# First guess of 1/Q in a PSUM bank: MoE1's reciprocal without VectorE operations on two SBUF operands

## The chip, the cores and the metric

The kernel runs on one core of a Trainium2 chip. The metric is the device time of one launch in microseconds. The engines are TensorE (PE, with its weight loads listed as PEld), VectorE (DVE), ScalarE (ACT), GpSimd (POOL) and SyncE (SP, which only issues DMAs here). Each engine runs its own instructions in the order in which the program wrote them, and waits on semaphores for the others. SBUF is the large on-chip memory, PSUM the small one into which TensorE writes its products.

## The reference

Three layers follow each other on 2304 tokens of width 512:

```
x = attention(q, k, v)                      # 4 batches, 8 heads, local and strided masks
h = x @ w_in                                # MoE1: 512 -> 2048
P = a0 + a1 h + a2 h^2 + a3 h^3
Q = 1 + |b0| |h| + |b1| h^2
x = (P / (Q + 1e-6)) @ w_out                # 2048 -> 512
out = gate * (relu(x @ w1[e]) @ w2[e])      # MoE2: e = the token's best expert of 8
```

All is float32. The products of MoE1 and MoE2 are made of three products each, with every operand split into a high part, which TensorE takes at full speed, and a low part, the rest.

## The kernel before

MoE1 is a pipeline over 96 steps. Step s is one block of 384 tokens (s // 16, six blocks) and one chunk of 128 hidden units (s % 16). One step is:

- **m1** (line 499): 12 matmuls of 384 columns into one of the two PSUM banks of tag "h".
- **fA** (446, 447), ScalarE: A = |h|, and G = a line in h, both to SBUF.
- **fP** (451, 452), GpSimd: Q = (b1 A + b0) A.
- **fD**, **fE** (457, 462), VectorE: G = G h and G = (G + a1) h. The h here is read from PSUM, and after fE its bank is free.
- **rA** (466, 467), ScalarE: A = Ln(Q + c), then A = Exp(-A): the first guess of 1/Q. The constant c is 1 + 1e-6.
- **rD**, **rN**, **rG** (471, 475, 479), VectorE: Q = (Q + c) A, Q = (Q - 2) A (one Newton step), G = (G + a0) Q.
- **sA** (383), ScalarE: gh, the high part of G. **sP** (489), GpSimd or VectorE: gl = G - gh.
- **m2** (510): 9 matmuls of 512 columns into three PSUM banks of tag "o".

The tiles A, Q, G, gh and gl have two buffers each. The order in which the program writes its operations is an order written by hand: `PLAN` has one line of operation names for each phase, and a window takes it through two steps. An entry such as `rA@-1` in window w means "go on with rA to step 2w - 1", and it is passed over where `ready` says that what it needs has not been written yet; a later entry of the same name then catches up. The phases are "first" (windows 0 to 7), "plain" (8 to 14), "attention" (15 to 31) and "last" (from 32). Attention of the first batch runs ahead of step 0, that of the second within steps 0 to 15, and that of the last two within steps 30 to 63. So steps 16 to 29 and 64 to 95 have no attention beside them. What they have is the router of MoE2 (rT, rE, rL, rP, rQ, rB: TensorE transposes and small products, with evacuations by ScalarE and VectorE), in the last phase also the sorting of tokens by expert (`rank`, `star_keys`, `star_slots`) and the splitting of MoE2's first weights (`w_unit`, lines 1097 and 1098).

In the phase "plain" one window is written as

```
m2@-3 rA@-1 m1@0 fA@0 xA.A@-2 sc@0 rD@-1 rN@-1 rG@-1 fP.G@0 ae.A@-1 lq@0 sA.A@-1 m1@1 mid@0 fD@0
fE@0 mx@0 rL@1 rP.A@1 rE.D@1 sP.D@-1 qk.A@1 rA@0 rT@0 m2@-2 rB@0 rD@0 rN@0 rG@0 mid@1 tail@1 aT@0
fA@1 fD@1 fE@1 sA.A@0 tail@0 rc@0 fP.G@1 end@1 xD@-1 nm.G@0 pv@0 sP.G@0 ex.A@0 end@0 rQ@1
```

All other PSUM work after the start-up (transposes, scores, router) takes its bank from `misc`, which goes round three banks of tag "m". A bank taken with a name is held until `release` of that name; `can_alloc(k)` says whether the next k banks in the round have been released, and `ready` asks it for the operations that need one.

Of the kernel before, what the change touches and what calls it, by code (L numbers as in the profile page):

```python
# [19 lines left out]
def tile_attention_moe_moe2(  # L20
# [86 lines left out]

# [1 line left out]
    pairs = [(b, hp) for b in range(B) for hp in (0, 2, 1, 3)]  # L109
# [51 lines left out]

# [1 line left out]
    ident = const.tile([128, 128], F32, name="ident")  # L163
# [19 lines left out]

    # coefficients: columns 0-3 = -a, 4-5 = |b|, 6 = 1 + 1e-6
    coef = const.tile([128, 8], F32, name="coef")
# [5 lines left out]

# [1 line left out]
    wi = w_in.bitcast(U32).rearrange("(k p) w -> p k w", p=128)  # L193
# [72 lines left out]

# [1 line left out]
    qkT = {}  # L268
# [30 lines left out]
    def emit_scores(U):  # L299
        n, hf = UN[U]  # L300
        hp = pairs[n][1]
        nq, nk, cnt = shape_of(U)
        qT, kT = qkT[n, "q"], qkT[n, "k"]
        banks = [misc('sc'), misc('sc')]
        where = {}
        for c in range(cnt):
            for j in range(2):
                if hp < 2:
                    # rows: head j's d; columns: position
                    r, o = j, c * nk  # L310
                    q0 = 96 * (hf * cnt + c)
                    k0 = max(q0 - 32, 0)
                else:
                    # rows: d for even or odd residues; columns: head, residue pair, position
                    r, o = c % 2, (2 * j + c // 2) * nk
                    q0 = k0 = 288 * hf + o
                PE.matmul(
                    banks[r][0:nq, o : o + nk],
                    lhsT=qT[64 * r : 64 * r + 64, q0 : q0 + nq],
                    rhs=kT[64 * r : 64 * r + 64, k0 : k0 + nk],  # L320
                    start=True, stop=True,
                )
                where[c, j] = banks[r][0:nq, o : o + nk]
        sc_t[U] = where
# [108 lines left out]

# [1 line left out]
    xs = dram.tile([NT, XW], F32, name="xs")  # L435
    hid = {}
    st = {}
# [21 lines left out]
    def ew_p2(s):  # L459
        A, Q, G = st[s]  # L460
        h = hid.pop(s)
        DVE.scalar_tensor_tensor(out=G, in0=G, scalar=coef[:, 1:2], in1=h, op0=ALU.add, op1=ALU.mult)  # L462

    def ew_recip(s):
        A, Q, G = st[s]
        ACT.activation(out=A, in_=Q, func=ACTF.Ln, bias=coef[:, 6:7])  # L466
        ACT.activation(out=A, in_=A, func=ACTF.Exp, scale=-1.0)  # L467

    def ew_newton(s):
        A, Q, G = st[s]  # L470
        DVE.scalar_tensor_tensor(out=Q, in0=Q, scalar=coef[:, 6:7], in1=A, op0=ALU.add, op1=ALU.mult)  # L471

    def ew_newton2(s):
        A, Q, G = st[s]
        DVE.scalar_tensor_tensor(out=Q, in0=Q, scalar=2.0, in1=A, op0=ALU.subtract, op1=ALU.mult)  # L475

    def ew_ratio(s):
        A, Q, G = st[s]
        DVE.scalar_tensor_tensor(out=G, in0=G, scalar=coef[:, 0:1], in1=Q, op0=ALU.add, op1=ALU.mult)  # L479

# [31 lines left out]

# [1 line left out]
    wg = px.tile([128, KD * E + 32 - E], F32, name="wg")  # L514
# [34 lines left out]
    def route_mm(i, t):  # L549
        """Parts of the logits: rows 32 k to 32 k + 7 for the k-th 128 of the model dimension (other rows unused)."""  # L550
        xT = x2t[i, t, "s"]
        m = x2t[i, t, "P"] = misc("rL")
        for kk in range(KD):
            PE.matmul(m[32 * kk : 32 * kk + 32, 0:128], lhsT=wg[:, E * kk : E * kk + 32],
                      rhs=xT[:, 128 * kk : 128 * kk + 128], start=True, stop=True, tile_position=(0, 32 * kk))
# [18 lines left out]
    def first_max(dst, src, n):  # L574
        """dst <- one-hot of the first maximum along the last axis of src [128, n, E]; returns src - max."""
        mx = px.tile([128, n, 1], F32, tag="mx", name="mx", bufs=2)
# [31 lines left out]

# [1 line left out]
    NU = len(UN)  # L610
# [5 lines left out]

    # The order of the work: one line of operations for each phase, as name[.engine]@offset. In the start-up an
    # operation goes on to attention unit (or weight group) u + offset; later, a window is two steps of MoE1, and an
    # operation goes on to step 2 w + offset, or to the unit of window w + offset.
    # MoE1: m1 m2 products, fA fP fD fE polynomials, rA rD rN rG reciprocal and ratio, sA sP high and low part of the result.  # L620
    # Attention: qk q and k transposed, sc scores, mx maximum, ex exponential, rc nm division by the sum, aT ae transposed
    # weights, pv values, xA xD high and low part of the result. c0A c0P c1 c1b c2A c2P: conversion of weights; lw, lq, ln:
    # loads; rT rE rL rP rQ rB: router; x0 x1 y0 y1: start of MoE2's first tile; kw: idle products; mid, tail, end: work of MoE2's routing.
    PLAN = {
# [33 lines left out]
    PLAN = {name: list(parse(text)) for name, text in PLAN.items()}  # L658
    CV = (1, 0, 2, 1, 2, 1, 3, 1, 2, 4, 1)   # weight units whose conversion starts, by iteration of the start-up
    LD = (2, 6, 0, 0, 0, 6, 0, 2, 1, 0, 0)   # weight units whose load starts  # L660
    KW = ((13, 0, 0), (0, 2, 11), (0, 1, 5), (1, 2, 4), (2, 0, 3), (6, 0, 2), (0, 3, 9), (0, 9, 0), (5, 3, 7), (8, 7, 0), (0, 9, 4))
    B0 = 1

# [1 line left out]
    NS = NBLK * NF  # L665
# [26 lines left out]
    def ready(T, j):  # L692
# [21 lines left out]
        elif T == "aT":  # L714
            return can_alloc(2)
        elif T in ("pv", "rL", "rQ"):
            return can_alloc(1)
# [48 lines left out]
    def releasing(f, kind, n):  # L766
# [6 lines left out]
        "x0": lambda j: x_T(0), "x1": lambda j: x_evac(0), "y0": lambda j: up(0, 0), "y1": lambda j: up(0, 1),  # L773
        "m1": mm1, "fA": ew_abs, "fP": ew_q, "fD": ew_p, "fE": ew_p2, "rA": ew_recip, "rD": ew_newton, "rN": ew_newton2, "rG": ew_ratio, "sA": ew_high,
        "sP": lambda s, eng: ew_low(s, DVE if s == NS - 1 else eng), "m2": run_m2, "sc": emit_scores, "mx": releasing(emit_max, "sc", 2), "ex": emit_exp,
# [95 lines left out]

# [1 line left out]
    R = {}  # L873
# [36 lines left out]
    def cols(x, n, m):  # L910
        """x [128, n] seen as [128, n, m]."""
        return x.rearrange("p (n o) -> p n o", o=1).to_broadcast([128, n, m])

    def rows(x, n, m):
        """x [128, m] seen as [128, n, m]."""
        return x.rearrange("p (o m) -> p o m", o=1).to_broadcast([128, n, m])
# [12 lines left out]
    def rank(i, eng):  # L929
        """Rank of each token among its expert's tokens, as (row of 128, place in it)."""  # L930
        rank_mm(i)
# [21 lines left out]
    def choose():  # L953
        """The expert with the most tokens so far: its weights are loaded early."""
        s = small_t([128, 1, E], "star")
# [13 lines left out]
    def reserve():  # L969
        """Tile 0 takes the chosen expert's tokens up to here; later ones start at tile 1."""  # L970
        c = R["cum"][:, 15]
        DVE.scalar_tensor_tensor(out=c, in0=R["s"], scalar=float(TILE), in1=c, op0=ALU.mult, op1=ALU.max)

    def index_tiles(m, n, name):
        """m [128, 2n] in PSUM: place + 1, and token tile, of each slot (0: empty) -> gather and scatter rows."""
        vv, v, z = small_t([128, 2 * n], name + "vv"), small_t([128, n], name + "v"), small_t([128, n], name + "z")
# [8 lines left out]
    def star_keys(i0, i1):  # L985
        """Rows of 128 of the chosen expert's tokens, others negative, for blocks i0 to i1 - 1."""
        tt, n = slice(3 * i0, 3 * i1), 3 * (i1 - i0)
# [10 lines left out]
    def star_slots(a, i0, i1):  # L998
        """Columns of tile a (0 or 1): place + 1, and token tile, of blocks i0 to i1 - 1."""
        tt = slice(3 * i0, 3 * i1)  # L1000
# [51 lines left out]
    def experts():  # L1052
        """Expert of each tile, and the number of tiles."""
        m, b = R["tiles"]
# [21 lines left out]
    def load_e(t, k):  # L1076
        """Expert weights of tile t, matrix k (1 or 2), as four slots."""
        e = R["e", t]
# [55 lines left out]
    def hidden(t, f):  # L1134
        """High and low part of a chunk of the hidden units; the first of tile 0 lie where MoE1's last block was."""
        if t == 0 and f < KD:
# [54 lines left out]

    # the router's later half inside MoE1
    last = NBLK - 1
    at_step(end, 63, route_setup)
    def spread(s0, g, every=1):
        """One part of g per step, from step s0 on."""
        def part():
# [158 lines left out]
```

## Time and profile before

| what | value |
|---|---|
| median of 3 runs | 891.7 us (891.23 to 892.05) |
| span of the profiled execution, from its first to its last instruction | 887.6 us |
| median of the runs less that span | 4.1 us |
| busy share of the span: PE, DVE, ACT, POOL | 91%, 82%, 60%, 54% |
| mean granted TensorE clock | 0.964 of full |

The profile is that of one execution. Its span leaves out what lies ahead of the first and behind the last instruction, so it stands below the runs' times. Matmuls are pipelined: each is listed with some 340 to 400 ns, but the next one starts before it ends, so that the distance from start to start, not the listed duration, is what a matmul costs.

### The profile page before, as it was taken

What the parts mean: (1) busy time and instruction counts of PE and PEld (TensorE: products, weight loads), DVE (VectorE), ACT (ScalarE), POOL (GpSimd) and SP (SyncE); (2) the same over time, 40 slices, a digit from 0 to 9 for tenths busy, and PEclk for the clock granted to TensorE, in tenths of its full rate; (3) what the DMA queues carried; (4) which work ended last, traced back from release to release, by engine and by line L of the source; (5) the groups of instructions that cost most, each with busy time, mean ns of one, the idle gap of its engine ahead of it and who ended that gap; (6) DMA issues with size and microseconds to landing.
All of it is one profiled execution on the core that took longest, in us unless ns stands there. A gap on an engine that the chain in (4) does not pass through costs nothing.

```text
span 887.6 us, 15602 instructions
## 1 busy us (share of the span) xinstructions
PE 804.6 (91%) x5294; PEld 677.4 (76%) x5301; DVE 730.9 (82%) x1656; ACT 534.4 (60%) x1397; POOL 476.8 (54%) x463
## 2 busy tenths in 40 slices
PE   6787787889999999999999988997899999999995
PEld 3555676767878788888788867886679999999994
DVE  5899999889897988788988999889966677777772
ACT  4776676565556887888776545555542555555552
POOL 3786878785554444443446667666613444444431
PEclk9888898899999999999999999999999999999998
DMA  8991241102000211131000000302014877776730
GB/s 197 304 271 47 75 126 45 31 8 64 8 1 28 80 44 35 27 105 35 20 15 25 12 1 1 131 1 97 24 38 114 340 238 232 226 232 223 231 120 5
DMA packets 71609, 85.59 MB, mean 96 GB/s; under 512 B 38111, under 2 KB 48607, under 8 KB 71520
## 3 DMA queue, kind: packets, MB, share of 16 engines
q1 hardware_dynamic: 68112, 74.36, 27.6%
q0 software_dynamic: 3120, 10.13, 3.4%
q8 instruction: 44, 0.72, 0.3%
q14 instruction: 45, 0.37, 0.1%
q10 hardware_dynamic: 288, 0.00, 0.0%
HBM read 74.89 MB, written 9.85 MB: 95 GB/s over the span
## 4 chain that ended last, share of the span: by engine, by line
PE 38%; DVE 29%; ACT 12%; POOL 8%; issue 6%; DMA 3%; SPq 2%; another core or an unknown queue 0%; DVEq 0%; POOLq 0%; ACTq 0%
PE h L1147 12%; PE o L1161 11%; DVE G L479 7%; DVE Q L475 6%; PE h L499 5%; PE o L510 5%; DVE Q L471 5%; ACT S L353 3%; ACT A L466 3%; ACT A L467 3%; POOL Q L452 3%; POOL Q L451 2%; DVE G L457 1%; POOL S L370 1%; DVE G L462 1%
## 5 line engine op out<-in xcount | busy, mean ns | idle before, releaser
L499 PE MATMUL h<-xh,wi 128*128 128x384 f32 x768 | 221.5, 351 | 7.5 <-DVE G L462 7.0
L510 PE MATMUL o<-wo,gh 128*128 128x512 f32 x576 | 190.9, 413 | 4.3 <-ACT gh L383 2.4
L451 POOL TENSOR_SCALAR Q<-A,coef 128x384 f32<-128x384 f32 x96 | 86.0, 896 | 163.5 <-ACT A L446 163.2
L499 PEld LDWEIGHTS h<-xh,wi 128*128 128x128 f32 x768 | 145.1, 194 | 13.8 <-DVE G L462 11.0
L499 PE MATMUL h<-xl,wi 128*128 128x384 f32 x384 | 132.1, 344 | 4.7 <-DVE xl L432 4.7
L510 PEld LDWEIGHTS o<-wo,gh 128*128 128x128 f32 x576 | 106.1, 192 | 30.7 <-ACT gh L383 6.3
L510 PE MATMUL o<-wo,gl 128*128 128x512 f32 x288 | 118.4, 411 | 5.5 <-POOL gl L489 3.2
L452 POOL TENSOR_TENSOR Q<-Q,A 128x384 f32<-128x384 f32 x96 | 111.8, 1164 | 8.0
L383 ACT CAST gh<-G 128x384 fp32r<-128x384 f32 x96 | 49.2, 512 | 103.9 <-DVE G L479 103.7
L489 POOL TENSOR_TENSOR gl<-G,gh 128x384 fp32r<-128x384 f32 x71 | 74.7, 1052 | 46.6 <-ACT gh L383 43.3
L471 DVE SCALAR_TENSOR_TENSOR Q<-Q,coef,A 128x384 f32<-128x384 f32 x96 | 66.0, 688 | 33.7 <-ACT A L467 23.1
L479 DVE SCALAR_TENSOR_TENSOR G<-G,coef,Q 128x384 f32<-128x384 f32 x96 | 90.7, 945 | 3.4
L1147 PE MATMUL h<-xh,w1h 128*128 128x256 f32 x320 | 89.7, 280 | 1.6 <-DVE G L462 1.6
L1147 PE MATMUL h<-xh,w1l 128*128 128x256 f32 x320 | 89.1, 278 | 0.0
L1147 PE MATMUL h<-xl,w1h 128*128 128x256 f32 x320 | 88.9, 278 | 0.0
L1151 ACT ACTIVATE hh<-h 128x256 fp32r<-128x256 f32 x76 | 29.2, 384 | 98.9 <-PE h L1147 98.9
L353 ACT ACTIVATE S<-S,nb 72x72 f32<-72x72 f32 (+1 forms) x224 | 80.6, 363 | 6.8 <-DVE nb L340 6.8
L466 ACT ACTIVATE A<-Q,coef 128x384 f32<-128x384 f32 x96 | 59.0, 615 | 36.6 <-POOL Q L452 36.5
L499 PEld LDWEIGHTS h<-xl,wi 128*128 128x128 f32 x384 | 74.8, 195 | 6.6 <-DVE xl L432 5.0
L475 DVE SCALAR_TENSOR_TENSOR Q<-Q,A 128x384 f32<-128x384 f32 x96 | 76.9, 801 | 3.3
L510 PEld LDWEIGHTS o<-wo,gl 128*128 128x128 f32 x288 | 55.5, 193 | 26.7 <-POOL gl L489 9.7
L1152 DVE SCALAR_TENSOR_TENSOR hl<-h,hh 128x256 fp32r<-128x256 f32 x76 | 32.2, 424 | 39.7 <-ACT hh L1151 39.7
(208 smaller groups left out, 1879.0 us busy)
## 6 DMA issues: line engine op xcount, KB each, us to landing
w1r<-in_moe_w_dram SPq DMA_DIRECT2D x36, 512.0 KB
w2r<-in_moe_w_dram SPq DMA_DIRECT2D x36, 512.0 KB
rawi<-in_moe_w_in_dram SPq DMA_DIRECT2D x16, 512.0 KB
rawo<-in_moe_w_out_dram SPq DMA_DIRECT2D x16, 512.0 KB
xs<-x SPq DMA_DIRECT2D x18, 256.0 KB
vt<-in_v_dram SPq DMA_DIRECT2D x48, 64.0 KB
rawq<-in_q_dram SPq DMA_DIRECT2D x16, 144.0 KB
rawk<-in_k_dram SPq DMA_DIRECT2D x16, 144.0 KB
```

The costliest lines, as they stand in the source:

```text
L353: ACT.activation(out=Sv[:, j, c], in_=Sv[:, j, c], func=ACTF.Exp, scale=-1.0, bias=nb[0:nq, u : u + 1], **({"accum_out": rb[0:nq, u : u + ...
L451: eng.tensor_scalar(out=Q, in0=A, scalar1=coef[:, 5:6], scalar2=coef[:, 4:5], op0=ALU.mult, op1=ALU.add)
L452: eng.tensor_tensor(out=Q, in0=Q, in1=A, op=ALU.mult)
L466: ACT.activation(out=A, in_=Q, func=ACTF.Ln, bias=coef[:, 6:7])
L471: DVE.scalar_tensor_tensor(out=Q, in0=Q, scalar=coef[:, 6:7], in1=A, op0=ALU.add, op1=ALU.mult)
L475: DVE.scalar_tensor_tensor(out=Q, in0=Q, scalar=2.0, in1=A, op0=ALU.subtract, op1=ALU.mult)
L479: DVE.scalar_tensor_tensor(out=G, in0=G, scalar=coef[:, 0:1], in1=Q, op0=ALU.add, op1=ALU.mult)
L489: eng.tensor_tensor(out=gl, in0=G, in1=gh.bitcast(F32), op=ALU.subtract)
L499: PE.matmul(h[:, 0:BLK], lhsT=w[:, o + 128 * kk : o + 128 * kk + 128], rhs=x[:, kk, c0 : c0 + BLK], start=n == 0, stop=n == 11)
L510: PE.matmul(acc[t], lhsT=a[:, ts], rhs=w[:, o : o + 512], start=f == 0 and n == 0, stop=f == NF - 1 and n == 2)
L1147: PE.matmul(h, lhsT=w[kk][:, 128 * f : 128 * f + 128], rhs=x[:, kk, c0 : c0 + TILE], start=n == 0, stop=n == 11)
L1161: PE.matmul(acc, lhsT=a[:, hs], rhs=w[f // 2][:, ws], start=f == 0 and n == 0, stop=f == NH - 1 and n == 2)
```

## The change

In steps 16 to 29 and 64 to 95 (46 of 96) `ew_recip` takes a bank of tag "m" under the name "y", and the Exp writes the first guess y there instead of into A. The three VectorE operations are written in another order of factors: G = (G + a0) y, then y = (Q + c) y within the bank, then G = (y - 2) G, after which the bank is released. The number of operations, their kinds, their sizes and their engines stay as they were. Each of the three now has one tensor operand in PSUM and one in SBUF, and the second one also writes to PSUM. In `ready`, rA of such a step asks for a free bank, and rD, which now needs G, for fE of its step. The other 50 steps keep the old form, and `PLAN` is not touched. The rest of the diff takes out comments.

```
+    def y_in_psum(s):
+        return 16 <= s < 30 or s >= 64
+
     def ew_recip(s):
         A, Q, G = st[s]
         ACT.activation(out=A, in_=Q, func=ACTF.Ln, bias=coef[:, 6:7])
-        ACT.activation(out=A, in_=A, func=ACTF.Exp, scale=-1.0)
...
+        y = misc("y")[:, 0:BLK] if y_in_psum(s) else A
+        ACT.activation(out=y, in_=A, func=ACTF.Exp, scale=-1.0)
+        st[s] = y, Q, G
+
+    def ew_1(s):
+        y, Q, G = st[s]
+        if y_in_psum(s):
+            DVE.scalar_tensor_tensor(out=G, in0=G, scalar=coef[:, 0:1], in1=y, op0=ALU.add, op1=ALU.mult)
+        else:
+            DVE.scalar_tensor_tensor(out=Q, in0=Q, scalar=coef[:, 6:7], in1=y, op0=ALU.add, op1=ALU.mult)
+
+    def ew_2(s):
+        y, Q, G = st[s]
+        if y_in_psum(s):
+            DVE.scalar_tensor_tensor(out=y, in0=Q, scalar=coef[:, 6:7], in1=y, op0=ALU.add, op1=ALU.mult)
+        else:
+            DVE.scalar_tensor_tensor(out=Q, in0=Q, scalar=2.0, in1=y, op0=ALU.subtract, op1=ALU.mult)
+
+    def ew_3(s):
+        y, Q, G = st[s]
+        if y_in_psum(s):
+            DVE.scalar_tensor_tensor(out=G, in0=y, scalar=2.0, in1=G, op0=ALU.subtract, op1=ALU.mult)
+            release("y")
+        else:
+            DVE.scalar_tensor_tensor(out=G, in0=G, scalar=coef[:, 0:1], in1=Q, op0=ALU.add, op1=ALU.mult)
...
-        elif T in ("pv", "rL", "rQ"):
+        elif T == "rD":
+            return not y_in_psum(j) or done["fE"] > j
+        elif T in ("pv", "rL", "rQ") or (T == "rA" and y_in_psum(j)):
             return can_alloc(1)
...
-        "m1": mm1, "fA": ew_abs, "fP": ew_q, "fD": ew_p, "fE": ew_p2, "rA": ew_recip, "rD": ew_newton, "rN": ew_newton2, "rG": ew_ratio, "sA": ew_high,
+        "m1": mm1, "fA": ew_abs, "fP": ew_q, "fD": ew_p, "fE": ew_p2, "rA": ew_recip, "rD": ew_1, "rN": ew_2, "rG": ew_3, "sA": ew_high,
```

## Rows read from the trace of the kernel before

**Rows 1.** Windows: stretch, length; busy us (count) of PE, PEld, DVE, ACT, POOL; clock, DMA.

```profile
210.00:280.00 70.00, 66.50 (x347) 55.39 (x346) 60.78 (x98) 39.74 (x84) 36.16 (x36) 0.98 0.11 32
478.00:600.00 122.00, 115.62 (x607) 95.37 (x605) 110.51 (x199) 66.50 (x139) 81.20 (x86) 1.00 0.09 31
600.00:645.00 45.00, 36.80 (x195) 29.75 (x195) 42.80 (x88) 25.79 (x53) 28.85 (x27) 1.00 0.19 60
```

**Rows 2.** Chain that ended last, one step of block 1: start, us, what.

```profile
247.07 0.40 issue
247.47 0.62 ACT A L466
...
248.11 0.54 ACT A L467
...
248.74 0.63 DVE Q L471
...
249.39 0.92 DVE Q L475
...
250.34 1.25 DVE G L479
```

**Rows 3.** Timeline of DVE and POOL: start, us, engine, line, operation.

```profile
249.98 1.20 POOL L452 TENSOR_TENSOR Q<-Q,A 128x384 f32<-128x384 f32 x1
...
275.53 0.62 DVE L479 SCALAR_TENSOR_TENSOR G<-G,coef,Q 128x384 f32<-128x384 f32 x1
...
276.12 0.66 POOL L451 TENSOR_SCALAR Q<-A,coef 128x384 f32<-128x384 f32 x1 [1.91 <-ACT A L446]
```

**Rows 4.** One line's instructions: shortest, median and longest in ns, first and last start.

```profile
L462 DVE SCALAR_TENSOR_TENSOR G<-G,coef,h x96: 601/614/617, 86.2 to 640.1; 128x384 f32<-128x384 f32 x96
...
L1152 DVE SCALAR_TENSOR_TENSOR hl<-h,hh x76: 410/425/426, 655.3 to 871.7; 128x256 fp32r<-128x256 f32 x76
```

**Rows 5.** Timeline of PE around 590 us: start, us, engine, line, operation, count.

```profile
586.14 0.60 PE L539 MATMUL m<-ident,x 128*128 128x128 f32 x4
...
586.76 0.34 PE L499 MATMUL h<-xl,wi 128*128 128x384 f32 x1
...
588.49 0.34 PE L499 MATMUL h<-xh,wi 128*128 128x384 f32 x1
...
589.69 0.40 PE L510 MATMUL o<-wo,gl 128*128 128x512 f32 x1
...
593.19 0.40 PE L510 MATMUL o<-wo,gl 128*128 128x512 f32 x1
```

**Rows 6.** PE busy time (count) in the stretches of rows 1: line 499, then line 510.

```profile
210.00:280.00 70.00, 30.63 (x163) 0.98 0.11 32
478.00:600.00 122.00, 56.40 (x296) 1.00 0.09 31
600.00:645.00 45.00, 13.86 (x72) 1.00 0.19 60
...
210.00:280.00 70.00, 33.94 (x126) 0.98 0.11 32
478.00:600.00 122.00, 58.97 (x225) 1.00 0.09 31
600.00:645.00 45.00, 19.47 (x74) 1.00 0.19 60
```

**Rows 7.** A PE wait at 266 us (timeline), and PE and its clock just after (windows).

```profile
266.46 1.06 PE L290 MATMUL m<-ident,rawk 72*128 72x72 f32 x8 [0.85 <-ACT x2T L383]
...
268.00:269.00 1.00, 1.00 (x4) 0.50 0.54 70
```

**Rows 8.** DVE busy time (count) from 600 to 645 us: lines 471, 475, 479.

```profile
600.00:645.00 45.00, 5.77 (x8) 1.00 0.19 60
...
600.00:645.00 45.00, 5.55 (x8) 1.00 0.19 60
...
600.00:645.00 45.00, 7.84 (x8) 1.00 0.19 60
```

More of the change, by code (lines that the diff above doesn't have):

```diff
@@ L466, in ew_recip @@
         ACT.activation(out=A, in_=Q, func=ACTF.Ln, bias=coef[:, 6:7])
-        ACT.activation(out=A, in_=A, func=ACTF.Exp, scale=-1.0)
[L469 to L479, printed above, removed]
+        y = misc("y")[:, 0:BLK] if y_in_psum(s) else A
[20 more added lines that the diff above has]
+            DVE.scalar_tensor_tensor(out=G, in0=G, scalar=coef[:, 0:1], in1=Q, op0=ALU.add, op1=ALU.mult)
     def ew_high(s, eng=ACT):
```

## The prediction

> **What bounds the kernel now.** I read the table of stretches first, then the chain of waits inside one stretch, then the timeline of two engines, and last the counts of matmuls.
>
> The 46 changed steps lie in two places: steps 16 to 29 between 210 and 280 us, and steps 64 to 95 between 478 and 645 us. There VectorE is busy 60.8 of 70, 110.5 of 122 and 42.8 of 45 us [rows 1]. TensorE looks full in the same rows (66.5 of 70), but a listed matmul overlaps the next, so its busy time hides short waits. From start to start it costs less: between 586.76 and 588.49 us lie ten starts of 384 columns, 0.173 us each; between 589.69 and 593.19 fifteen of 512 columns, 0.233 us each [rows 5]. A step of MoE1 (12 and 9 of them) is thus 12 x 0.173 + 9 x 0.233 = 4.18 us of TensorE at best.
>
> The chain of waits shows why a step takes longer than that. Near 247 us it never touches TensorE: ScalarE casts G of one step (sA), then takes the Ln and Exp of the next (rA), VectorE does rD, rN and rG, and the cast of that step waits for rG. ScalarE's order is sA(s), rA(s+1), fA(s+2), sA(s+1), so this is a closed loop. From the cast's wait at 247.07 to rD at 248.74 pass 1.67 us; the three VectorE operations last until 250.34 + 1.25 = 251.59, 2.85 us; 0.05 us pass to the next cast: 4.57 us a step [rows 2], against 4.18 of TensorE.
>
> In that loop rN takes 0.92 and rG 1.25 us [rows 2]. The same rG at 275.53 us, where POOL idles (its next operation starts at 276.12 after 1.91 us of idleness), takes 0.62; the slow rG runs beside POOL's multiplication of 249.98, 1.20 us long [rows 3]. So VectorE and GpSimd hold each other up where both read from SBUF. VectorE's operations with one operand in PSUM don't suffer: fE (line 462), of the same kind and size, stays within 601 to 617 ns in all 96 cases, and line 1152, whose first operand is in PSUM and whose second is in SBUF, within 410 to 426 in 76 [rows 4], although POOL is busy for over half of the span.
>
> **The change part by part.** *The three VectorE operations.* The new rD is fE's form to the letter (SBUF tensor, coefficient, PSUM tensor): 0.61 us. The new rG is line 1152's form with 384 columns instead of 256. I price each of the three at 0.62, the free rG [rows 3], and 0.65 with the gap behind it: 1.95 us for 2.85. The loop becomes 1.67 + 1.95 + 0.05 = 3.67 us, under TensorE's 4.18, so in a step without other work TensorE is next to bind.
>
> *Writing to PSUM.* The Exp and the middle operation write to PSUM, which no ScalarE or VectorE row here does. From below: the fastest similar operation is line 1152's 0.43 us, which would change little, since TensorE binds already. From above I take the contended rG, 1.25 us [rows 2]: the loop is then 3.67 + 0.63 = 4.30. I take 0.62, because reading PSUM costs nothing extra (0.61 in fE against 0.62 from SBUF [rows 3, 4]); both ends stay in the range. The Exp by itself has over half a microsecond of room (4.18 - 3.67).
>
> [...]
>
> *The bank.* y holds one of three "m" banks from rA to rG. Of the entries between these two in the plan, none in "plain" or "last" takes more than one bank (rT, one `rank` product) before rG releases y, and in the phase "last" rE gives rT's bank back before the next rA; the two banks of x0 are asked for after one y, with the other two free. So I find no place where rA is put off. The real wait is that an Exp writes where three allocations earlier another user sat: mostly y of two or three steps before, whose rG is over long since. Behind a late Exp would queue fA and sA of ScalarE, and for these VectorE and POOL. In window 14 the second q transpose takes the bank of y(27), so TensorE now waits there for rG(27); but the evacuations of these transposes already stand behind sA(27), which needs the same rG, and that is why TensorE waits 0.85 us at 266 us [rows 7]. No wait is new in length.
>
> *rD after fE.* fE(s) is written ahead of rD(s) in every window of both phases, so the condition is always met. Costs nothing.
>
> *POOL.* Its operations lose the same collisions: 1.20 us for the Q product [rows 3]. It isn't in the loop: no gain counted. DMAs are not touched.
>
> *The sum*, by how much TensorE waits in each stretch. The floor is the counts of matmuls [rows 6] times 0.173 and 0.233; the other matmuls get 0.08 us each (four transposes and a product lie between 586.14 and 586.76, so 0.11 each; one product, eight small ones and two of 512 columns between 588.49 and 589.69, so 0.07 each [rows 5]).
> - 210 to 280: 163 x 0.173 + 126 x 0.233 + 58 x 0.08 = 62.2, so 7.8 us of waiting. After the wait at 266 us the granted clock is at its lower level, 0.50 or 1.2 GHz [rows 7], and eight matmuls take about twice as long: some 1.6 us, which I leave standing, with half of the wait ahead of it, 0.7. Gain 5.5.
> - 478 to 600: 296 x 0.173 + 225 x 0.233 + 86 x 0.08 = 110.5, so 11.5 us. VectorE sheds 25 x 0.9 = 22 us at most, far more than that. But routing work sits in the chains of VectorE and POOL here, and its waits don't go. I take 70%, my choice: 8.0.
> - 600 to 645: 72 x 0.173 + 74 x 0.233 + 49 x 0.08 = 33.6, so 11.4 us. Here VectorE is full (42.8 of 45 [rows 1]), with the splitting of weights on it. The three lines take 5.77 + 5.55 + 7.84 = 19.2 us [rows 8]; eight steps at 3 x 0.62 are 14.9. VectorE still binds, and the gain is what it sheds: 4.3.
>
> Together 17.8 us. Nothing later gives it back: attention and MoE2 keep their code and simply start earlier. Against the span of 887.6 that is 869.8; the runs stand 4.1 us above the span, so the median goes from 891.7 to about 874.0.
>
> **The rivals.**
> *The writes are dear* (rN near 1.25 us). The loop is 4.30 instead of 4.57: 14 x 0.27 = 3.8 us in the first stretch, 25 x 0.27 = 6.8 in the second, cut by the same 70% to 4.7, and 4.3 - 8 x 0.63 = -0.7 in the third: 7.8 us, 884. For it: no row of such a write. Against it: reading is free of any extra.
>
> *Slower: writes into PSUM that cost more than the collisions did.* Place: the Exp and rN, both in the loop. The point that decides is 2.85 - 1.95 = 0.90 us a step more than I priced; at 1.2 us more, 46 x 0.3 = 13.8 us are lost: 905.5. Against it: it would need a threefold price for an operation whose read side shows none.
>
> *No change: TensorE binds already.* For it: near 590 us, with router work between the products, its starts follow each other without a gap [rows 5]. If all steps were like that, faster VectorE would only wait longer, and the time would stay within 1.8 us of 891.7. Against it: 7.8 + 11.5 + 11.4 = 30.7 us in which TensorE waits.
>
> *All waiting goes*, the clock's dip and the routing's waits with it: at most 30.7, say 27 us: 864.7.
>
> **How the numbers follow.** The forecast, with a gain of 11 to 25 us (867 to 881), gets 0.70; dear writes 0.12; all waiting gone 0.06; no change 0.05; slower 0.07. The range 864 to 885 takes in the forecast, the dear writes at the upper bound and most of the largest gain; it leaves out some 0.15. A measurement here can tell about 0.2%, 1.8 us, from no change. Faster by more: 0.70 + 0.12 + 0.06 = 0.88; same 0.05; slower 0.07.
>
> **What the profile after would show.** Right: rG and rN of the changed steps at 0.56 to 0.65 us whether or not POOL works beside them; the chain between 210 and 265 us through TensorE instead of lines 471 to 479; VectorE's busy share there down from 87% to about 75%; TensorE's waits for fE and gl shorter; steps 30 to 63 as they were. Wrong: an Exp well over 0.54 us or a middle operation over 1 us; an Exp waiting for a bank; a new dip of the clock; or waits of the routing chain in 478 to 645 us as long as now, so that the second and third gains shrink.

## The result, and the profile after

The changed kernel takes 865.8 us (864.46 to 866.58), beside 891.47 for the kernel before in the same comparison: a ratio of 0.9711, with a 95% interval of 0.9698 to 0.9725, so 25.7 us less. The forecast was 874.0 us, 17.8 less. The direction and the mechanism held, and the time lies inside the stated range of 864 to 885. But it lies 1.2 us below the forecast's own range (867 to 881), and the case nearest to it is the one in which all waiting goes (864.7).

The page of the changed kernel: busy time of each engine, and the chain that ended last, by engine and by line.

```profile
PE 793.3 (92%) x5301; PEld 678.0 (79%) x5301; DVE 688.3 (80%) x1656; ACT 536.6 (62%) x1397; POOL 464.1 (54%) x463
...
PE 55%; DVE 19%; ACT 11%; POOL 7%; issue 4%; DMA 2%; SPq 0%; another core or an unknown queue 0%; POOLq 0%; DVEq 0%; ACTq 0%
PE h L516 13%; PE o L527 12%; PE h L1166 12%; PE o L1180 11%; ACT S L353 4%; DVE G L496 3%; DVE Q L488 2%; POOL Q L452 2%; DVE Q L481 2%; POOL Q L451 2%; ACT A L470 2%; POOL S L370 1%; ACT A L472 1%; PE m L379 1%; PE zb L632 1%
```

The same line of the chain on the page of the kernel before:

```profile
PE 38%; DVE 29%; ACT 12%; POOL 8%; issue 6%; DMA 3%; SPq 2%; another core or an unknown queue 0%; DVEq 0%; POOLq 0%; ACTq 0%
```

TensorE's part of the chain rose to 55%, from 38%, and VectorE's fell to 19%, from 29%.

The table of stretches, with the columns of [rows 1]. Each window now reaches from the start of one step's Ln to that of another (steps 16 to 30, 64 to 88, 88 to 95), so that both kernels are compared over the same steps. The kernel before:

```profile
209.50:277.91 68.41, 64.91 (x336) 53.78 (x335) 59.47 (x96) 38.18 (x78) 35.21 (x36) 0.98 0.12 32
480.68:600.72 120.04, 113.31 (x596) 93.26 (x594) 108.55 (x199) 66.49 (x139) 79.82 (x85) 1.00 0.09 32
600.72:640.43 39.71, 32.25 (x172) 26.12 (x170) 37.89 (x78) 22.57 (x47) 27.61 (x27) 1.00 0.21 68
```

The changed kernel:

```profile
210.21:271.63 61.42, 60.86 (x336) 53.20 (x335) 46.32 (x96) 38.83 (x78) 30.81 (x36) 1.00 0.13 36
474.75:581.56 106.81, 106.72 (x587) 93.10 (x587) 86.76 (x199) 67.87 (x139) 72.79 (x85) 1.00 0.10 36
581.56:616.40 34.84, 32.98 (x185) 28.44 (x184) 33.46 (x78) 22.64 (x45) 25.93 (x27) 1.00 0.23 77
```

In the first two VectorE is now busy for 75% and 81% of the time (87% and 90% before) and TensorE for over 99%. In the third VectorE is still at 96%.

The Exp and the three VectorE operations in the changed steps (shortest, median, longest in ns; the first row is the Exp of the 50 other steps, into SBUF):

```profile
L472 ACT ACTIVATE A<-A x50: 522/525/529, 85.5 to 470.8; 128x384 f32<-128x384 f32 x50
L472 ACT ACTIVATE m<-A x46: 495/496/497, 210.9 to 617.0; 128x384 f32<-128x384 f32 x46
...
L479 DVE SCALAR_TENSOR_TENSOR G<-G,coef,m x46: 599/612/616, 211.4 to 617.6; 128x384 f32<-128x384 f32 x46
...
L486 DVE SCALAR_TENSOR_TENSOR m<-Q,coef,m x46: 609/617/618, 211.9 to 618.1; 128x384 f32<-128x384 f32 x46
...
L493 DVE SCALAR_TENSOR_TENSOR G<-m,G x46: 556/557/559, 212.6 to 618.8; 128x384 f32<-128x384 f32 x46
```

Before, the second and the third of the three operations, over all 96 steps:

```profile
L475 DVE SCALAR_TENSOR_TENSOR Q<-Q,A x96: 557/742/1560, 87.8 to 642.8; 128x384 f32<-128x384 f32 x96
...
L479 DVE SCALAR_TENSOR_TENSOR G<-G,coef,Q x96: 617/902/1568, 88.3 to 643.4; 128x384 f32<-128x384 f32 x96
```

Not one of the 138 VectorE operations of the changed steps is longer than 618 ns. The middle one, which also writes to PSUM, costs as much as one that writes to SBUF (medians of 617 ns, and of 618 for Q = (Q + c) A in the 50 other steps of this profile, line 481), and the Exp is 29 ns shorter into PSUM (496 against 525 ns).

The chain of waits in block 1 (start, us, what) no longer leaves TensorE:

```profile
214.85 2.61 PE h L516 x15
217.46 0.43 PE m L556 x4
217.89 4.19 PE o L527 x18
222.08 4.16 PE h L516 x24
226.25 4.20 PE o L527 x18
230.44 1.56 PE h L516 x9
```

A window of two steps is 4.16 + 4.20 = 8.36 us, that is 4.18 a step: the price that the prediction worked out for a full TensorE. Before, the chain there was the loop of [rows 2].

The transposes at which TensorE had waited for 0.85 us and after which its clock fell [rows 7] now wait for less, and in this profile the clock stays at full speed (1.00). The timeline:

```profile
262.30 0.47 PE L290 MATMUL m<-ident,rawk 72*128 72x72 f32 x4 [0.26 <-ACT qT L383]
```

and the window behind it, of TensorE alone:

```profile
263.00:264.00 1.00, 1.00 (x6) 1.00 0.52 172
```

The gain by steps comes from the starts of the Ln of steps 16, 30, 64, 88 and 95 (line 466 before, 470 after), differences in us. Each row is one execution, the profiled one. The kernels of the experiments stand in the same table.

```
kernel                        16 to 30   30 to 64   64 to 88   88 to 95
before                            68.4      202.8      120.0       39.7
changed                           61.4      203.1      106.8       34.8
e1_sbuf                           67.2      202.9      119.4       41.1
e2_old_order                      63.0      202.9      111.5       38.2
e3_no_middle                      61.4      202.8      106.8       33.9
e4_one_more                       61.4      202.8      114.0       38.4
e5_block1                         61.4      202.8      120.0       40.5
e6_from56                         61.4      203.9      107.5       36.5
e7_wider                          61.1      201.7      107.5       36.5
e8_fp_dve                         73.2      203.6      124.3       40.9
e9_after                          61.4      203.1      106.8       34.9
e10_wider                         61.1      201.7      107.5       34.9
e11_from62                        61.1      202.0      107.5       34.8
```

The change brings 7.0, 13.2 and 4.9 us in its three stretches, 25.1 in all, and attention between them keeps its time.

### The profile page after: what moved, and what is told of

Its sections match the earlier page's. It is cut to its first block, busy times and chain, and to the rows that moved or that the text cites. A ratio compares the mean times of both kernels' runs of the same rounds, so it can differ in the third digit from the quotient of the medians.

```text
span 862.7 us, 15597 instructions
## 1 busy us (share of the span) xinstructions
PE 793.3 (92%) x5301; PEld 678.0 (79%) x5301; DVE 688.3 (80%) x1656; ACT 536.6 (62%) x1397; POOL 464.1 (54%) x463
## 4 chain that ended last, share of the span: by engine, by line
PE 55%; DVE 19%; ACT 11%; POOL 7%; issue 4%; DMA 2%; SPq 0%; another core or an unknown queue 0%; POOLq 0%; DVEq 0%; ACTq 0%
PE h L516 13%; PE o L527 12%; PE h L1166 12%; PE o L1180 11%; ACT S L353 4%; DVE G L496 3%; DVE Q L488 2%; POOL Q L452 2%; DVE Q L481 2%; POOL Q L451 2%; ACT A L470 2%; POOL S L370 1%; ACT A L472 1%; PE m L379 1%; PE zb L632 1%
## 5 line engine op out<-in xcount | busy, mean ns | idle before, releaser
L516 PE MATMUL h<-xh,wi 128*128 128x384 f32 x768 | 219.2, 350 | 1.3 <-DVE G L462 1.3
L527 PE MATMUL o<-wo,gh 128*128 128x512 f32 x576 | 188.8, 409 | 2.1 <-POOL wo L249 1.8
L451 POOL TENSOR_SCALAR Q<-A,coef 128x384 f32<-128x384 f32 x96 | 80.3, 837 | 188.1 <-ACT A L446 187.8
L527 PE MATMUL o<-wo,gl 128*128 128x512 f32 x288 | 116.3, 404 | 0.9 <-POOL gl L506 0.5
L452 POOL TENSOR_TENSOR Q<-Q,A 128x384 f32<-128x384 f32 x96 | 103.5, 1079 | 8.0
L516 PEld LDWEIGHTS h<-xl,wi 128*128 128x128 f32 x384 | 74.9, 195 | 6.6 <-DVE xl L432 5.0
L446 ACT ACTIVATE A<-h 128x384 f32<-128x384 f32 x96 | 46.5, 485 | 40.6 <-PE h L516 40.4
L457 DVE TENSOR_TENSOR G<-G,h 128x384 f32<-128x384 f32 x96 | 52.3, 545 | 17.1 <-ACT G L447 17.1
L447 ACT ACTIVATE G<-h,coef 128x384 f32<-128x384 f32 x96 | 63.9, 665 | 0.1
```

Of the source, the lines that this page charges most:

```text
L447: ACT.activation(out=G, in_=h, func=ACTF.Identity, scale=coef[:, 3:4], bias=coef[:, 2:3])
L451: eng.tensor_scalar(out=Q, in0=A, scalar1=coef[:, 5:6], scalar2=coef[:, 4:5], op0=ALU.mult, op1=ALU.add)
L452: eng.tensor_tensor(out=Q, in0=Q, in1=A, op=ALU.mult)
L457: DVE.tensor_tensor(out=G, in0=G, in1=h, op=ALU.mult)
L516: PE.matmul(h[:, 0:BLK], lhsT=w[:, o + 128 * kk : o + 128 * kk + 128], rhs=x[:, kk, c0 : c0 + BLK], start=n == 0, stop=n == 11)
L527: PE.matmul(acc[t], lhsT=a[:, ts], rhs=w[:, o : o + 512], start=f == 0 and n == 0, stop=f == NF - 1 and n == 2)
```

## The experiments

Ratios are to the kernel before, run on the same chip in the same comparison. The medians of before there were 893.6 to 894.7 us, so ratios, not microseconds, are compared with 0.9711.

### Where y lies, and the order of the factors

The first kernel keeps the new order of factors and puts y back into SBUF. No bank is taken, asked for or released.

```
-        y = misc("y")[:, 0:BLK] if y_in_psum(s) else A
+        y = A
...
-            release("y")
...
-        elif T in ("pv", "rL", "rQ") or (T == "rA" and y_in_psum(j)):
+        elif T in ("pv", "rL", "rQ") or False:
```

> The new order of factors in the 46 steps, with y in SBUF (tile A) instead of a PSUM bank; no bank is taken. Theory (two SBUF operands of VectorE collide with GpSimd): the collisions come back, with operations of 0.9 and 1.25 us among the three, and the time is that of the kernel before, within 3 us of 891.5. Rival (the new order of factors, or the earlier end of Q's use, brought the gain): most of the gain stays, 866 to 872 us.

Measured: 0.9972 (0.995 to 0.9993). The three operations in the 46 steps:

```profile
L479 DVE SCALAR_TENSOR_TENSOR G<-G,coef,A x46: 605/619/1368, 211.5 to 642.2; 128x384 f32<-128x384 f32 x46
...
L486 DVE SCALAR_TENSOR_TENSOR A<-Q,coef,A x46: 617/837/1418, 212.3 to 642.9; 128x384 f32<-128x384 f32 x46
...
L493 DVE SCALAR_TENSOR_TENSOR G<-A,G x46: 557/1253/1261, 213.1 to 643.6; 128x384 f32<-128x384 f32 x46
```

With the same algebra and the same order of work, the medians are back at 0.84 and 1.25 us, and a tenth of the gain is left. What counts is where y lies.

One thing does not come back with the waits. At the transposes of [rows 7] TensorE waits about as long as before, but its clock stays full:

```profile
266.45 1.05 PE L290 MATMUL m<-ident,rawk 72*128 72x72 f32 x8 [0.79 <-ACT x2T L383]
...
268.00:269.00 1.00, 1.00 (x6) 0.79 (x5) 0.00 (x0) 1.00 (x3) 0.00 (x0) 1.00 0.52 96
```

Its first stretch, with all collisions and no dip of the clock, takes 67.2 us, 1.2 less than that of the kernel before.

The second kernel leaves y in its bank and takes the old order of factors, in which only the last operation has two operands in SBUF.

```
+        DVE.scalar_tensor_tensor(out=Q, in0=Q, scalar=coef[:, 6:7], in1=y, op0=ALU.add, op1=ALU.mult)
...
+        DVE.scalar_tensor_tensor(out=Q, in0=Q, scalar=2.0, in1=y, op0=ALU.subtract, op1=ALU.mult)
...
+        DVE.scalar_tensor_tensor(out=G, in0=G, scalar=coef[:, 0:1], in1=Q, op0=ALU.add, op1=ALU.mult)
```

> y in the PSUM bank as in the changed kernel, but the three operations in the old order of factors, so that Q = (Q + c) y and Q = (Q - 2) y have one SBUF tensor each and G = (G + a0) Q has two. Theory (collisions): the first two stay at 0.56 to 0.62 us, the last one collides and takes up to 1.25. The loop of ScalarE and VectorE is then 1.67 + 0.65 + 0.60 + 1.28 + 0.05 = 4.25 us against 4.18 of TensorE, so a part of the gain stays where TensorE binds, and less where VectorE binds: 869 to 878 us. Rival (it is the PSUM bank as such, by a quicker Exp or freer SBUF tiles): 866 us as in the changed kernel.

Measured: 0.9835 (0.9787 to 0.9883), so 57% of the gain. Its three operations (the third row counts all 96 steps):

```profile
L478 DVE SCALAR_TENSOR_TENSOR Q<-Q,coef,m x46: 600/614/616, 212.6 to 628.7; 128x384 f32<-128x384 f32 x46
...
L482 DVE SCALAR_TENSOR_TENSOR Q<-Q,m x46: 553/554/556, 213.3 to 629.4; 128x384 f32<-128x384 f32 x46
...
L486 DVE SCALAR_TENSOR_TENSOR G<-G,coef,Q x96: 617/850/1572, 88.5 to 630.0; 128x384 f32<-128x384 f32 x96
```

The two with y don't exceed 616 ns. The one without it does, up to 1572, and from step 16 to 30 its 14 instructions take 15.1 us, 1.08 each. So the quick Exp or the freer SBUF tiles, which this kernel has too, don't bring the gain by themselves; what they add was not measured apart. The new order of factors matters because it lets all three meet y.

### Is GpSimd the other party?

In the kernel before, fP of the 46 steps is moved from GpSimd to VectorE; all tiles stay in SBUF.

```
-        "fP": ew_q,
+        "fP": lambda s, eng: ew_q(s, DVE if 16 <= s < 30 or s >= 64 else eng),
```

> The kernel before with fP of the 46 steps on VectorE instead of GpSimd, all tiles in SBUF as before. Theory (the other party of the collision is GpSimd's reading): with fP gone from GpSimd, the operations of the 46 steps fall from medians of 0.91 and 1.25 us to 0.56 and 0.62, except beside the gl subtraction that stays on GpSimd; VectorE has two more operations (some 0.9 to 1.2 us a step) and sheds about as much: 875 to 892 us. Rival (VectorE slows itself, by its own order or by ScalarE's reads): the medians stay, VectorE has over 5 us a step, and the time rises beyond 915 us.

Measured: 1.0089 (1.0058 to 1.012). One line's instructions over all 96 steps:

```profile
L475 DVE SCALAR_TENSOR_TENSOR Q<-Q,A x96: 557/558/1557, 88.1 to 654.0; 128x384 f32<-128x384 f32 x96
...
L479 DVE SCALAR_TENSOR_TENSOR G<-G,coef,Q x96: 617/619/1576, 88.7 to 654.6; 128x384 f32<-128x384 f32 x96
```

and the busy times from 215 to 272 us, with the columns of [rows 1]:

```profile
215.00:272.00 57.00, 49.19 (x263) 41.63 (x261) 48.95 (x88) 29.99 (x59) 5.24 (x6) 1.00 0.11 31
```

With GpSimd at 5.2 of 57 us the same operations, still with two SBUF operands, have medians of 558 and 619 ns over all 96 steps, against 742 and 902 before. From step 16 to 30 their means are 0.56 and 0.64 us, against 0.86 and 1.21 before. So GpSimd's work is the other half of the collision: with two operands in SBUF rG takes 1.25 us beside it and 0.62 without it [rows 2, 3], and with one operand in PSUM no operation of the changed steps exceeds 618 ns beside it. Where in the chip the two engines meet, no run shows.

The time, however, met neither expectation (it is some 8 us above the kernel before). I had counted VectorE's load, and overlooked that fP precedes rA: in the chain of waits of this kernel fP now stands on VectorE behind the previous step's rG, so both lie in the loop. Two pieces of it:

```profile
225.46 0.57 DVE Q L452
...
226.11 0.63 ACT A L466
```

### What binds now

The third kernel leaves out the middle operation of the 46 steps, and with it the Newton step.

```
-            DVE.scalar_tensor_tensor(out=y, in0=Q, scalar=coef[:, 6:7], in1=y, op0=ALU.add, op1=ALU.mult)
...
-            DVE.scalar_tensor_tensor(out=G, in0=y, scalar=2.0, in1=G, op0=ALU.subtract, op1=ALU.mult)
+            DVE.scalar_tensor_tensor(out=G, in0=y, scalar=0.0, in1=G, op0=ALU.mult, op1=ALU.subtract)
```

> The changed kernel without the middle operation y = (Q + c) y in the 46 steps; the third one is G = 0 y - G there. This leaves out the Newton step, so 1/Q is the first guess. It takes 0.64 us of VectorE out of each step. Theory (TensorE now binds in these steps): no more than 3 us below the changed kernel, 863 to 866 us, and what comes lies in the last eight steps. Rival (the loop through VectorE still binds): 46 x 0.64 = 29 us less, 840 us or below.

Measured: 0.9712 (0.9662 to 0.9762), the ratio of the changed kernel. Its middle and its last stretch:

```profile
475.10:581.88 106.78, 106.71 (x587) 93.09 (x587) 74.85 (x175) 67.89 (x139) 72.18 (x85) 1.00 0.10 36
581.88:615.80 33.92, 32.59 (x185) 28.59 (x184) 30.16 (x71) 22.70 (x46) 25.55 (x27) 1.00 0.25 79
```

VectorE has 12 us less to do in the middle stretch than in the changed kernel (74.9 against 86.8), and the stretch is as long: TensorE binds there. In the last seven steps VectorE sheds another 3.3 us (30.2 against 33.5) and only 0.9 come back. So in the changed kernel VectorE is not all that holds these steps. The chain of waits there runs through VectorE up to 602 us, then through a transfer that GpSimd starts (tokens for MoE2), and from 607 us on through TensorE:

```profile
601.93 1.62 POOL xg L1123
...
603.85 3.51 DMA xg<-xs,i0g
```

The fourth puts an operation of the same size in instead.

```
+            DVE.scalar_tensor_tensor(out=A, in0=Q, scalar=coef[:, 6:7], in1=y, op0=ALU.add, op1=ALU.mult)
             DVE.scalar_tensor_tensor(out=y, in0=Q, scalar=coef[:, 6:7], in1=y, op0=ALU.add, op1=ALU.mult)
```

> The changed kernel with one more operation of VectorE in the 46 steps, ahead of the middle one: A = (Q + c) y into the spare tile, 0.62 us, read by nobody. Theory (TensorE binds, with 4.18 us a step against 3.67 of the loop): the loop is 4.32 us, so at most 0.14 us are lost where no router work fills TensorE, and 0.65 a step in the last eight, where VectorE is nearly full: 3 to 10 us more, 869 to 876. Rival (the loop still binds): 46 x 0.65 = 30 us more, 895 us.

Measured: 0.9816 (0.9765 to 0.9867), 9.4 us above the changed kernel (0.0105 of 891.5). In its profile block 1 loses nothing, the middle stretch 7.2 us, the last one 3.6. VectorE is then busy for 52.3 of 61.4 us in block 1 and for 100.1 of 114.0 in the middle stretch. The timeline of TensorE at one of its waits:

```profile
543.77 0.73 PE L532 MATMUL o<-wo,gh 128*128 128x512 f32 x2 [1.39 <-ACT gh L383]
544.86 0.50 PE L532 MATMUL o<-wo,gl 128*128 128x512 f32 x1 [0.36 <-POOL gl L511]
```

and the window behind it, whose third number from the end is the granted clock:

```profile
546.00:549.00 3.00, 3.00 (x10) 2.71 (x9) 2.50 (x5) 1.42 (x3) 1.86 (x2) 0.50 0.00 0
```

Where the sorting of tokens stands between the steps, one more operation makes VectorE late for m2; TensorE waits 1.75 us, and then its granted clock is 0.50 for some 3 us: from 547.14 to 548.42 us its matmuls of 384 columns start 0.32 us apart, against 0.173 at full clock. So the changed kernel has room for less than one VectorE operation a step in steps 64 to 88.

### Does each stretch keep its gain?

The fifth kernel changes steps 16 to 29 alone.

```
-        return 16 <= s < 30 or s >= 64
+        return 16 <= s < 30
```

> The change in steps 16 to 29 alone; steps 64 to 95 keep the old form. Theory (each stretch gains by itself and nothing is given back): the gain of the first stretch alone, some 7 us as the step times of the two profiles show it, ratio to the kernel before 0.992. Rival (what the first stretch gains is given back at the start of attention or later, and the gain of the changed kernel is all from steps 64 to 95): no difference, ratio 1.000.

Measured: 0.9929 (0.9901 to 0.9956), 6.3 us. The table shows the 7.0 us of the first stretch. Attention and the middle stretch are those of the kernel before, so nothing is given back there. The last stretch is 0.8 us longer, with the clock at 0.50 near 627 us in this profile.

### More steps

The sixth takes y's bank from step 56 on, beside the last units of attention (`s >= 56` in place of `s >= 64`).

> The changed kernel with y in a PSUM bank from step 56 on, so also in eight steps beside the last attention units, which take two of the three banks at a time for scores and transposed weights. Theory (a held bank puts off what needs one; in these steps little collides, so there is nothing to gain): the scores, transposes or rA are put off by half a window in several of these steps, 2 to 12 us more than the changed kernel between steps 56 and 64. Rival (the third bank is enough): within 1 us of the changed kernel.

Measured: 0.9749 (0.9721 to 0.9777), 3.4 us above the changed kernel. From the Ln of step 56 to that of 58 its profile has 2.1 us more than that of the changed kernel. The timeline of TensorE at the q and k transposes there, in this kernel:

```profile
435.11 0.47 PE L290 MATMUL m<-ident,rawq 72*128 72x72 f32 x4 [1.01 <-DVE xl L432]
436.63 0.72 PE L290 MATMUL m<-ident,rawk 72*128 72x72 f32 x8 [1.04 <-ACT qT L383]
```

a window after them:

```profile
438.00:439.00 1.00, 1.00 (x4) 0.72 (x4) 0.18 (x1) 1.00 (x3) 0.67 (x1) 0.50 0.00 0
```

and in the changed kernel:

```profile
433.42 0.73 PE L290 MATMUL m<-ident,rawk 72*128 72x72 f32 x8 [0.88 <-DVE xl L432]
```

TensorE waits twice instead of once, and the clock falls to half. One more bank taken shifts the round, and by what ended these waits a transpose now meets a bank whose last reader is later; that reading was not tested by itself. It is the cost that I had expected of the held bank, but by a wait on the chip, not by an operation put off in the program. About 1.1 us come back up to step 64.

The rest lies in two places. From the Ln of step 65 to that of 66 there are 0.7 us more, as in e7 and e10 below. From 94 to 95 there are 1.7 more, with a dip of the clock at 612 us. e7 and e10 are one kernel, and e7's profile has the same 1.7 and a dip while e10's has neither. So this part can come and go with the execution and need not be the bank's.

The seventh adds the steps at the edges of the two stretches: `14 <= s < 31 or s >= 63`.

> The changed kernel with y in a PSUM bank also in steps 14, 15, 30 and 63, where the old form still shows collisions in steps 14, 15 and 63. Theory: 3 us of collisions lie in these steps, of which those at the edge of a stretch that waits for VectorE come back: 0.5 to 2 us less than the changed kernel. Rival (the attention of batch 1 or 2 beside them needs the bank): the same or up to 3 us more.

Measured: 0.9657 (0.963 to 0.9685). It was run again beside the changed kernel and beside a version that adds step 62.

> The changed kernel once more, beside two versions with more steps on the same chip: ratio to the kernel before 0.971 as at first.

> The version with steps 14, 15, 30 and 63 added, beside the changed kernel on the same chip. Theory (the gain seen in its steps 15, 16 and 64, 4 us in all, is real): ratio to the kernel before 0.966 to 0.967, 4 us below the changed kernel. Rival (its first comparison was chance): 0.971.

> As the version with steps 14, 15, 30 and 63, and step 62 too, which stands beside the end of the last attention unit. Theory (little collides in step 62, so nothing is left to gain): within 1 us of that version. Rival (a bank held there puts off the last values or weights of attention): 1 to 3 us more.

Measured: the changed kernel 0.9725 (0.9706 to 0.9745), the wider one 0.9682 (0.9659 to 0.9704), the one with step 62 0.9702 (0.9673 to 0.973). By medians that is 868.05, 864.84 and 864.82 us. The wider version beats both kernels, by 3.2 us over the changed one (4 were expected); step 62 adds nothing to the median, and its six runs spread from 863.1 to 870.1. In the seventh's profile the stretches from Ln to Ln that end at steps 15, 16 and 64 are shorter than in the changed kernel's by 2.6, 0.6 and 1.0 us, and the one that ends at 66 is 0.7 longer.

## Why the prediction was right, and what it mis-sized

**The collision.** Right. The operations fell to 0.56 to 0.62 us, and e1, e2 and e8 take the cause apart: two operands in SBUF (e1, e2), and GpSimd beside them (e8).

**The loop.** Right. In block 1 it vanished from the chain, and TensorE's 4.18 us a step took its place. It is even shorter than the 3.67 us that I priced. In the new order the first two operations don't need each other's result, and VectorE starts the second 0.53 us after the first, before its listed end. The three take 1.74 us from 222.45 us on, not 1.95, which makes 3.46 by the same sum, an estimate. That leaves room for e4's extra operation, which costs block 1 nothing.

**The price of writing to PSUM.** The value taken, 0.62 us, is what was measured (617 ns). The rival of dear writes and the one that was slower by them are out. Reading from PSUM costs nothing extra either: 612 ns with one operand there, 619 without (medians of L479 in the changed kernel and in e1).

**The bank.** Right for these 46 steps: no wait of an Exp for its bank shows. e6 shows that it would be wrong in steps 56 to 58, with attention beside; e10, which holds the bank in four steps at the edges, shows no such loss.

**GpSimd.** Right: its operations lost the collisions too. The Q product (line 452) took 16.5 us in the 14 steps from 16 to 30 before and takes 14.3 now.

**The sum.** Here the step failed that leaves waiting in place; the mechanism stood, and the sizes were too small, above all in the middle stretch.
- 210 to 280 us, 5.5 forecast, 7.0 measured. I left 1.6 us standing for the clock's dip, and in the changed kernel's profile there is none. No trace gives the forecast's 1.2 GHz as a frequency: that of the kernel before shows a granted clock of 0.50 and, from 267.97 to 270.53 us, matmuls of 512 columns that start 0.427 us apart, or 1.2 columns a ns, against 0.233 us at full clock, so that eight of them cost 1.6 us more. Whether the shorter wait took it away is open: in e1 the wait is back at 0.79 us and there is no dip either. Against e1's 67.2 us, also without a dip, the gain is 5.7, close to the forecast.
- 478 to 600, 8.0 forecast, 13.2 measured: the term "I take 70%, my choice". I took the waits of routing for chains of their own. They were places in VectorE's line. In these 24 steps the three operations went from 63.3 us to 42.8, VectorE's other work hardly changed (45.3 before, 44.0 after), and with room in the line the routing was absorbed: TensorE's listed busy time there is 106.72 of 106.81 us. e3 and e4 bracket it, with nothing to gain from less and 7.2 us to lose from one more. The waiting itself, 11.5 us by the floor, was also a little under-counted.
- 600 to 645, 4.3 forecast, 4.9 measured: VectorE bound there, as said, and the gain is what the three lines shed in the seven steps, from 17.4 to 12.5 us. That VectorE still binds after the change holds only in part: of the 3.3 us that e3 takes off it, 0.9 come back.

**The rivals.** "No change" needed a TensorE without waits, and 13 us of waits went in the middle stretch alone. "All waiting goes", which I gave 0.06, was nearest to the result.

## What to carry to other kernels

Where VectorE sets the pace beside a busy GpSimd, look for two-operand operations whose duration jumps between two values (here 0.62 and 1.25 us), and move one operand to PSUM, choosing the order of factors so that every operation meets it. To size the gain, compare per stretch the next engine's full load with the new sum of the relieved engine. Where the sum stays well below it, small work queued on the relieved engine can be absorbed too, and no share of the waits need be held back: here VectorE's 86.8 us beside TensorE's 106.8. That the sum fits is not enough: at e4's 100.1 us 7.2 were lost. Stop where the banks are in use by others: e6 lost 3.4 us there.

## What was not expected of the hardware

- A short stall of TensorE can cost more than itself, but need not. Before the change a wait of 0.85 us at 266 us was followed by the lower clock [rows 7]; in e4 waits of 1.39 and 0.36 us, and in e6 of 1.01 and 1.04, were followed by 0.50 for some 3 us. But e1's 0.79 us at 266 us and the changed kernel's 0.88 at 433 were not. In e7 and e10, the same kernel, TensorE waits for the same transfer near 603 and 601 us, 0.74 and 0.56 us at first and then as listed, and only e7's clock falls. That makes e7's stretch from step 94 to 95 1.6 us longer than e10's. What decides it is open. The second wait and the clock behind it, e7 first:

```profile
604.39 0.98 PE L1139 MATMUL m<-ident,xg 128*128 128x128 f32 x7 [1.03 <-DMA xg<-xs,i0g]
...
606.00:607.00 1.00, 1.00 (x4) 0.50 0.00 0
...
602.29 0.98 PE L1139 MATMUL m<-ident,xg 128*128 128x128 f32 x7 [1.13 <-DMA xg<-xs,i0g]
...
604.00:605.00 1.00, 1.00 (x7) 1.00 0.00 0
```

- VectorE pays nothing for a PSUM destination in this form (617 ns, in place, against 618 from and into SBUF), and ScalarE's Exp into PSUM is 29 ns shorter than into SBUF (496 against 525).
